# Batch 1 loaded two and three tokens a partition, with transposes, loads and copies moved, in a sliding-window attention and GEGLU kernel

## The chip, the cores and the metric

One core of one Trainium2 chip. The metric is the device time of one execution in microseconds (us). An execution takes some 1.8 us more than the span that its profile shows (366.16 us for a span of 364.4). A run is called slow here when it is over 1.5% above the fastest of its kernel; verdicts use fast runs. Clock means the clock granted to PE, the matmul engine (TensorE), as a share of full speed.

## The reference

Eight batches of attention (8 heads, 576 tokens, head size 64), with an ALiBi bias and a window of 128 tokens, feed one feed-forward block over all 4608 tokens.

```python
scores = scale * np.matmul(q, k.transpose(0, 1, 3, 2))
mask = (rel >= 0) & (rel < 128)
scores = np.where(mask, scores + bias[None], -1e9)
attn = softmax(scores)                        # shortened
x = (attn @ v) as [4608, 512]                 # shortened
return (gelu(x @ w_gate) * (x @ w_val)) @ w_out
```

## The kernel before

It works in nine groups of 512 tokens: gate and value matmuls (`gate_val`), then eight half tiles of the output product (`out_half`), among which the attention of the next batches is placed by hand. PE is meant never to stop. ACT is ScalarE, DVE is VectorE, POOL is GpSimd, SP is SyncE. Batch 0 and batch 1 are transposed by PE, batches 2 to 7 by DMA transposes that SP issues. POOL issues all loads, in program order. `bank()` gives one PSUM bank. Cuts are marked.

```python
RUNS = ((0, 128, 3), (384, 96, 2))       # batch 0: first token, partitions, tokens a partition

def transpose_runs(n, what, c, ps):      # used for batch 0
    first, parts, r = RUNS[n]
    src = runs((qs, ks)[what][0], n)
    for x in range(r):
        for i in (0, 1):
            nc.tensor.transpose(out=ps[64 * i:64 * i + 64, parts * x:parts * x + parts],
                                in_=src[:, 2 * c + i, 64 * x:64 * x + 64], ...)

def untangle(copy, n, what, c, ps): ...  # strided copy of that PSUM tile to qT or kT

def transpose(b, what, c, copy):         # used for batch 1
    ps = bank().bitcast(BF16)
    for j in range(5):
        nc.tensor.transpose(out=ps[:, 128 * j:128 * j + 128],
            in_=(qs, ks)[what][b][:, j, 128 * c:128 * c + 128], identity=ident)
    copy(out=(qT, kT)[what][b][:, :, c, :], in_=ps[:, 0:640].rearrange(...))

# ... the loop over groups
for g in range(NG):
    for b in ((), (2, 3), (4,))[g] if g < 3 else ():
        transposes_dma(b)
    if g + 2 < B:
        load_v(g + 2)
    for f in range(7 if g == 0 else 0, NF):
        gate_val(g, f)
        if g == 0 and f in (9, 11):
            for c in (0, 1) if f == 9 else (2, 3):
                for w in (0, 1):
                    transpose(1, w, c, (act, dve)[w])
        if 2 <= g < B - 1:
            ...        # sums, spread_dma(g + 1) (the trip rd, rb), transposes_dma(g + 3), values
    for b in ((3,), (4, 5))[g] if g < 2 else (g + 4,):
        if b < B:
            load_qk(b)
    for item in steps(g):
        ...            # out_half, scores, sums, spread_pe, values
```

`spread_dma` writes a row of reciprocals to DRAM (`rd`) and reads it back spread over partitions (`rb`), which the product into `xT` needs.

The softmax here doesn't subtract the row's maximum and nothing guards it: scores larger than these inputs give would overflow.

Of the kernel before, what the change touches and what calls it, by code (L numbers as in the profile page):

```python
# [7 lines left out]
FP32 = mybir.dt.float32  # L8
# [18 lines left out]
def kernel(  # L27
# [10 lines left out]
    nc = tc.nc  # L38
    B, H, S, D = q.shape
    W = 128  # L40
    NTOK = B * S
    DM = H * D
    DFF = moe_w_gate.shape[1]
    NF = DFF // 128
    NG = NTOK // 512
# [11 lines left out]
    o_pool = ctx.enter_context(tc.tile_pool(name="op", bufs=3))  # L57
# [9 lines left out]
    def bank():  # L67
        ps = psum.tile([128, 512], FP32, name="ps")
        for _ in range(heat.pop()):
            nc.tensor.matmul(out=ps, lhsT=zeros[:, 0:128], rhs=zeros, start=True, stop=True)  # L70
        heat.append(0)
        return ps

    def keep_busy(n):
# [4 lines left out]
    wo = consts.tile([128, NF, DM], BF16, name="wo")  # L79
    xT = consts.tile([128, 4, NTOK], BF16, name="xT")  # L80
    ident = consts.tile([128, 128], BF16, name="ident")
# [4 lines left out]
    qs, ks = ([consts.tile([128, 5, DM], BF16, name=f"{nm}s{i}") for i in range(2)]  # L86
              for nm in "qk")
    qT, kT = ([consts.tile([128, 5, 4, 128], BF16, name=f"{nm}T{i}") for i in range(2)]
              for nm in "qk")
# [9 lines left out]
    def load_qk(b):  # L99
        load(qs[b % 2], q, b)  # L100
        load(ks[b % 2], k, b)
# [4 lines left out]
    def runs(t, n):  # L106
        first, parts, r = RUNS[n]
        lo = 1536 * n
        return t.rearrange("p j x -> p (j x)")[0:parts, lo:lo + 512 * r].rearrange(
            "p (h x) -> p h x", h=H)  # L110

    def load_runs(n, h0, h1):
        first, parts, r = RUNS[n]
        for t, src in ((qs[0], q), (ks[0], k)):
            nc.gpsimd.dma_start(
                out=runs(t, n)[:, h0:h1, :],
                in_=src[0][h0:h1, first:first + parts * r, :].rearrange(
                    "h (p r) d -> p h (r d)", r=r))

    def load_v(b, js=range(5)):  # L120
        load(vb[b % 2], v, b, js)
# [8 lines left out]
    def by_pair(t):  # L130
        return t.rearrange("p j c t -> p (j c t)").rearrange("p (c x) -> p c x", c=4)

    def transpose_runs(n, what, c, ps):

        first, parts, r = RUNS[n]
        src = runs((qs, ks)[what][0], n)
        for x in range(r):
            for i in (0, 1):
                nc.tensor.transpose(
                    out=ps[64 * i:64 * i + 64, parts * x:parts * x + parts],  # L140
                    in_=src[:, 2 * c + i, 64 * x:64 * x + 64],
                    identity=ident[0:parts, 0:parts])

    def untangle(copy, n, what, c, ps):

        first, parts, r = RUNS[n]
        dst = by_pair((qT, kT)[what][0])[:, c, 64 + first:64 + first + parts * r]
        if isinstance(c, int):
            copy(out=dst.rearrange("p (x r) -> p x r", r=r),  # L149
                 in_=ps[:, 0:parts * r].rearrange("p (r x) -> p x r", r=r))  # L150
        else:
            n = c.stop - c.start
            copy(out=dst.rearrange("p c (x r) -> p c x r", r=r),
                 in_=ps[:, 0:n * parts * r].rearrange("p (c r x) -> p c x r", c=n, r=r))

    def transpose(b, what, c, copy):
        ps = bank().bitcast(BF16)
        for j in range(5):
            nc.tensor.transpose(
                out=ps[:, 128 * j:128 * j + 128],  # L160
                in_=(qs, ks)[what][b][:, j, 128 * c:128 * c + 128], identity=ident)
        copy(out=(qT, kT)[what][b][:, :, c, :],
             in_=ps[:, 0:640].rearrange("p (j t) -> p j t", t=128))

    def blocks(t, b, i, c, j, n):
        if b == 0:
            return by_pair(t[b])[64 * i:64 * i + 64, c, 128 * j:128 * (j + n)].rearrange(
                "p (n t) -> p n t", n=n)
        return t[b % 2][64 * i:64 * i + 64, j:j + n, c, :]
# [126 lines left out]
    hid = {}  # L296
# [25 lines left out]
    def out_half(g, u):  # L322
        t, half = u // 2, u % 2
        if half == 0:
            acc[g] = bank()
        po = acc[g]
        for f in range(6 * half, 6 * half + 6):
            nc.tensor.matmul(  # L328
                out=po, lhsT=hid[g][:, f, 128 * t:128 * (t + 1)],
                rhs=wo[:, f, :], start=(f == 0), stop=(f == NF - 1))  # L330
        if half == 1:
            osb = o_pool.tile([128, DM], FP32, name="osb")
            nc.scalar.copy(out=osb, in_=po)  # L333
            r0 = 512 * g + 128 * t
            nc.sync.dma_start(out=out[r0:r0 + 128, :], in_=osb)


    load_runs(0, 0, 4)
    zeros = consts.tile([128, 512], BF16, name="zeros")
    nc.vector.memset(zeros, 0.0)  # L340
    nc.vector.memset(ident, 0.0)
    for t in (qT[0], kT[0]):
        nc.vector.memset(by_pair(t)[:, :, 0:64], 0.0)
    nc.vector.memset(sel, 0.0)
    nc.gpsimd.affine_select(
        out=ident, in_=ident, compare_op=ALU.not_equal, fill=1.0,
        base=0, pattern=[[-1, 128]], channel_multiplier=1)
    load_runs(0, 4, 8)
    tmpl = consts.tile([128, 256], FP32, name="tmpl")
    nc.gpsimd.iota(tmpl, pattern=[[1, 256]], base=0, channel_multiplier=-1,  # L350
                   allow_small_or_imprecise_dtypes=True)
    for half, base, step, chan in ((0, 0, 1, -1), (1, -1, -1, 1)):
        t = tmpl[:, 128 * half:128 * half + 128]
        nc.gpsimd.affine_select(
            out=t, in_=t, compare_op=ALU.is_ge, fill=1e9,
            base=base, pattern=[[step, 128]], channel_multiplier=chan)
    load_runs(1, 0, 8)
    step = DFF // 4
    load_v(0, (0, 1, 2))
    load_w(0, step)  # L360
    for c in range(4):
        nc.gpsimd.affine_select(
            out=sel, in_=sel, compare_op=ALU.not_equal, fill=1.0,
# [2 lines left out]
    load_v(0, (3, 4))  # L366
    for n in (2, 3):
        load_w(step * n, step * (n + 1))
    for t in (qs[1], ks[1]):
        nc.vector.memset(t[0:64, 0, :], 0.0)  # L370
    load_qk(1)


    nc.vector.memset(ones, 0.0)
# [11 lines left out]
    act, dve = nc.scalar.copy, nc.vector.tensor_copy  # L386
    def first(cs):
        for w in (0, 1):
            if w and len(cs) == 2:
                keep_busy(1)  # L390
            for c in cs:
                ps = bank().bitcast(BF16)
                transpose_runs(0, w, c, ps)
                untangle(dve, 0, w, c, ps)

    def rest(cs):
        for w in (0, 1):
            ps = bank().bitcast(BF16)
            for k, c in enumerate(cs):
                transpose_runs(1, w, c, ps[:, 192 * k:192 * k + 192])  # L400
            untangle(act, 1, w, slice(cs[0], cs[-1] + 1), ps)

    keep_busy(8)
    first((0, 1))
# [9 lines left out]
    masks, tails = [], []  # L414
# [23 lines left out]
    for n in range(2):  # L438
        nc.gpsimd.dma_start(
            out=wo[:, 6 * n:6 * n + 6, :],  # L440
            in_=moe_w_out[768 * n:768 * n + 768, :].rearrange("(c p) f -> p c f", p=128))
    load_v(1)
    for t in (qs[0], ks[0]):
# [6 lines left out]
    todo = {  # L450
        0: [("s2", 1), ("s", 1, 0, (0, 1)), 0, 1, ("s", 1, 0, (2, 3)), 2,
            ("s", 1, 1, (0, 1), None, masks), 3, ("sum", 1, 0), ("masks",),
            ("s", 1, 1, (2, 3)), 4, ("spread", 1, 0, (act, act)), 5, ("sum", 1, 1),
            ("pv", 1, 0), 6, ("spread", 1, 1, (act, act)), ("pv", 1, 1), 7],
        1: [("s2", 2), ("s", 2, 0, (0, 1)), 0, 1, ("s", 2, 0, (2, 3)), 2,
            ("s", 2, 1, (0, 1), None, masks), 3, ("sum", 2, 0), ("masks",),
# [9 lines left out]
    def steps(g):  # L466
        b = g + 2
        if g in todo:
            return todo[g]
        if b >= B:  # L470
            return range(8)
        return [("s2", b), ("s", b, 0, (0, 1)), 0, 1, 2, ("s", b, 0, (2, 3)),
                ("s", b, 1, (0,)), 3, 4, 5, ("s", b, 1, (1, 2, 3)), 6, 7]

    def flush():
        for args in masks:
# [1 line left out]
        masks.clear()  # L478

    RUN = {"s2": scores2, "s": scores, "sum": sums, "spread": spread_pe, "pv": values,  # L480
           "masks": flush}

    for g in range(NG):
        for b in ((), (2, 3), (4,))[g] if g < 3 else ():
            transposes_dma(b)
        if g + 2 < B:
            load_v(g + 2)
        for f in range(7 if g == 0 else 0, NF):
            gate_val(g, f)
            if g == 0 and f in (9, 11):  # L490
# [4 lines that stand above are left out]
                if f == (1 if g == 2 else 0):  # L495
                    sums(g + 1, 0)
                if f == (2 if g == 2 else 0):
                    sums(g + 1, 1)
                    spread_dma(g + 1)
                    if g + 3 < B:  # L500
                        transposes_dma(g + 3)
                elif g > 2 and f in (8, 10):
                    for s in (0, 1):
                        values(g + 1, s, (f - 8, f - 7))
        for b in ((3,), (4, 5))[g] if g < 2 else (g + 4,):
            if b < B:
                load_qk(b)
        for item in steps(g):
            if isinstance(item, int):
                out_half(g, item)  # L510
            else:
                RUN[item[0]](*item[1:])
# [30 lines left out]
```

## Time and profile before

| what | where it is read | value |
|---|---|---|
| time, 6 runs beside the change | times of the runs | 362.82 us median, 361.9 to 366.68 |
| profiled run | times of the runs | 366.16 us, counted as slow (1.9% above the fastest on record, 359.2) |
| PE busy | page, part 1 | 347.5 of 364.4 us |
| PE's longest wait | waits of PE | 3.2 us, for `xT` |

The prediction shows the lines. PE is the engine that matters, so a change is worth what it removes from PE's waits. One warning that the prediction did not take seriously enough: the only profile at hand was of a slow run, and its largest wait need not be there in a fast one.

### The profile page before, as it was taken

Reading aid. Unit: us, or ns where it says so; the run is one execution under the profiler, and the core shown is the slowest. Engines: PE = TensorE matmul, PEld = TensorE weight load, DVE = VectorE, ACT = ScalarE, POOL = GpSimd, SP = SyncE. Lnnn points to the kernel's source line nnn. Section 1 sums busy time; section 2 is a strip of 40 time slices with the busy share of each in tenths; the row PEclk is TensorE's granted clock in tenths of the full one; section 3 lists DMA queues with packets and bytes.
Section 4 is the critical chain, followed back from the end, with each engine's and each line's share of the span. In section 5 each row is a group of like instructions: output and inputs, shape, how many; then the busy total and the mean of one; then the engine's idle time right before and its main releaser. Section 6 shows DMA issues by size and latency. Waiting matters only on the chain.

```text
span 364.4 us, 6688 instructions
## 1 busy us (share of the span) xinstructions
PE 347.5 (95%) x2651; PEld 172.6 (47%) x2694; DVE 185.7 (51%) x301; ACT 187.2 (51%) x341; POOL 109.1 (30%) x140
## 2 busy tenths in 40 slices
PE   7799989999999999996999999999999999999995
PEld 2468544544454445443445444444444444444442
DVE  4887458434688646372547454655474404302420
ACT  4864495536977375631683368436842223323321
POOL 8956759913783073560400040000000000000000
PEclk9999999999999999999899999999999999999999
DMA  9999999999999999999921992060205020011002
GB/s 101 176 194 172 170 170 175 174 150 155 193 188 167 121 184 145 205 172 225 144 76 39 221 109 89 31 131 0 88 33 130 2 109 6 1 59 58 0 31 86
DMA packets 151728, 42.61 MB, mean 117 GB/s; under 512 B 138856, under 2 KB 144488, under 8 KB 151696
## 3 DMA queue, kind: packets, MB, share of 16 engines
q0 software_dynamic: 112608, 18.88, 68.4%
q1 hardware_dynamic: 39088, 23.30, 31.0%
q8 instruction: 21, 0.34, 0.4%
q14 instruction: 11, 0.09, 0.1%
HBM read 43.65 MB, written 9.53 MB: 146 GB/s over the span
## 4 chain that ended last, share of the span: by engine, by line
PE 61%; DMA 27%; POOL 4%; issue 2%; SPq 2%; DVE 2%; ACT 1%; POOLq 0%; ACTq 0%; DVEq 0%
PE ps L305 31%; PE ps L328 21%; DMA qT<-qs 7%; DMA wv<-in_moe_w_val_dram 6%; DMA qs<-in_q_dram 4%; DMA wo<-in_moe_w_out_dram 4%; PE ps L180 3%; PE ps L286 3%; DMA rb<-rd 2%; DMA out_dram<-osb 2%; SPq L173 2%; DMA vb<-in_v_dram 2%; PE ps L246 2%; DVE r L255 1%; DMA rd<-r 1%
## 5 line engine op out<-in xcount | busy, mean ns | idle before, releaser
L312 DVE TENSOR_TENSOR hT<-ps,gelu 128x512 bf16<-128x512 f32 (+2 forms) x115 | 74.0, 654 | 111.8 <-PE ps L305 97.8
L311 ACT ACTIVATE gelu<-ps 128x512 bf16<-128x512 f32 (+2 forms) x115 | 65.1, 571 | 119.1 <-PE ps L305 114.7
L305 PE MATMUL ps<-xT,wg 128*128 128x512 bf16 (+2 forms) x445 | 111.8, 368 | 1.0
L305 PE MATMUL ps<-xT,wv 128*128 128x512 bf16 (+2 forms) x452 | 111.5, 367 | 0.6
L328 PE MATMUL ps<-wo,hT 128*128 128x512 bf16 x414 | 97.5, 380 | 1.6 <-DMA wo<-in_moe_w_out_dram 0.8
L187 ACT ACTIVATE P<-ps 128x512 bf16<-128x512 f32 x144 | 73.7, 623 | 7.9 <-PE ps L180 7.6
L305 PEld LDWEIGHTS <-wv 128*128 128x128 bf16 x460 | 44.9, 98 | 49.7 <-issue 1.4
L305 PEld LDWEIGHTS <-wg 128*128 128x128 bf16 x460 | 43.4, 98 | 47.7 <-issue 1.4
L190 DVE TENSOR_TENSOR P<-P,emask 128x1024 bf16<-128x1024 bf16 x72 | 48.2, 692 | 34.7 <-ACT P L187 34.7
L328 PEld LDWEIGHTS <-hT 128*128 128x128 bf16 x432 | 39.9, 98 | 50.1 <-issue 5.1
L95 POOL DMA_DIRECT2D vb<-in_v_dram x40 | 33.8, 867 | 54.2 <-PE ps L286 51.6
L95 POOL DMA_DIRECT2D qs<-in_q_dram x35 | 29.5, 857 | 42.4 <-DMA qT<-qs 29.0
L333 ACT COPY osb<-ps 128x512 f32<-128x512 f32 x36 | 21.7, 603 | 34.7 <-PE ps L328 29.5
L255 DVE RECIPROCAL r<-ps 128x320 f32<-128x320 f32 (+1 forms) x16 | 30.7, 1938 | 5.3 <-PE ps L246 5.3
L95 POOL DMA_DIRECT2D ks<-in_k_dram x35 | 29.5, 868 | 8.2 <-DMA qs<-in_q_dram 3.2
L292 DVE TENSOR_TENSOR xT<-ps,rb 128x320 bf16<-128x320 f32 (+1 forms) x64 | 24.6, 446 | 7.2 <-DMA rb<-rd 6.5
L180 PE MATMUL ps<-qT,kT 64*128 64x256 bf16 (+1 forms) x384 | 21.8, 244 | 2.8 <-DVE kT L149 1.4
L286 PE MATMUL ps<-P,vb 128*64 128x128 bf16 (+2 forms) x384 | 18.8, 247 | 3.4 <-DVE xT L292 3.2
L180 PEld LDWEIGHTS <-kT 64*128 64x128 bf16 x384 | 13.1, 94 | 14.8 <-issue 10.3
L286 PEld LDWEIGHTS <-vb 128*64 128x64 bf16 x384 | 15.2, 111 | 9.1 <-issue 8.3
L246 PEld LDWEIGHTS <-ones 128*32 128x32 bf16 x384 | 7.6, 96 | 4.9 <-issue 4.3
L246 PE MATMUL ps<-P,ones 128*32 128x128 bf16 (+2 forms) x384 | 9.9, 243 | 0.0
(50 smaller groups left out, 89.2 us busy)
## 6 DMA issues: line engine op xcount, KB each, us to landing
out_dram<-osb SPq DMA_DIRECT2D x36, 256.0 KB, 2.0
rb<-rd SPq DMA_DIRECT2D x10, 576.0 KB, 7.4
vb<-in_v_dram POOLq DMA_DIRECT2D x32, 128.0 KB, 9.0
qs<-in_q_dram POOLq DMA_DIRECT2D x28, 128.0 KB, 7.2
ks<-in_k_dram POOLq DMA_DIRECT2D x28, 128.0 KB, 6.6
wg<-in_moe_w_gate_dram POOLq DMA_DIRECT2D x4, 384.0 KB, 9.1
wv<-in_moe_w_val_dram POOLq DMA_DIRECT2D x4, 384.0 KB, 10.1
wo<-in_moe_w_out_dram POOLq DMA_DIRECT2D x2, 768.0 KB, 11.3
```

Source lines behind the costliest of these rows:

```text
L95: nc.gpsimd.dma_start(out=t[lo:128, j, :].rearrange("p (h d) -> p h d", h=H), in_=src[b][:, 128 * j - 64 + lo:128 * j + 64, :].rearrange(" ...
L180: nc.tensor.matmul(out=ps[:, col:col + 128 * n].rearrange("p (n t) -> p n t", n=n), lhsT=blocks(kT, b, i, c, j, 1).rearrange("p n t -> p ( ...
L187: nc.scalar.activation(out=dst, in_=src, func=AF.Exp, scale=0.125)
L190: nc.vector.tensor_tensor(out=dst, in0=dst, in1=m, op=ALU.mult)
L246: nc.tensor.matmul(out=ps[32 * c:32 * c + 32, a:e], lhsT=ones[:, min(j, 1), i, :], rhs=prob(b, s, c, i, j, e - a), start=(i == 0 and j == ...
L255: nc.vector.reciprocal(sumrow[b][:, lo:hi], ps[:, 0:hi - lo])
L286: nc.tensor.matmul(out=ps[64 * i:64 * i + 64, a:e], lhsT=vb[b % 2][:, j, 64 * h:64 * h + 64], rhs=prob(b, s, c, i, j, e - a), start=(j == ...
L292: nc.vector.tensor_tensor(out=xT[:, c, b * S + lo:b * S + hi], in0=ps[:, 0:hi - lo], in1=recip[b][:, c, lo:hi], op=ALU.mult)
L305: nc.tensor.matmul(out=ps[:, 0:hi - lo], lhsT=w[:, c, 128 * f:128 * (f + 1)], rhs=xT[:, c, t0 + lo:t0 + hi], start=(c == 0), stop=(c == 3))
L311: nc.scalar.activation(out=gl[:, 0:hi - lo], in_=pg[:, 0:hi - lo], func=AF.Gelu)
L312: nc.vector.tensor_tensor(out=hid[g][:, f, lo:hi], in0=pv[:, 0:hi - lo], in1=gl[:, 0:hi - lo], op=ALU.mult)
L328: nc.tensor.matmul(out=po, lhsT=hid[g][:, f, 128 * t:128 * (t + 1)], rhs=wo[:, f, :], start=(f == 0), stop=(f == NF - 1))
```

## The change

The intent: fewer and longer pieces for batch 1's loads (3,584 in place of 9,216), so that what stands behind them in POOL's queue starts sooner; batch 2's transposes earlier; batch 7's loads out of the way of batch 4's reciprocals; some work moved from ScalarE to VectorE; a shorter tail.

```diff
     def transpose(b, what, c, copy):
         ps = bank().bitcast(BF16)
-        for j in range(5):
-            nc.tensor.transpose(
-                out=ps[:, 128 * j:128 * j + 128],
-                in_=(qs, ks)[what][b][:, j, 128 * c:128 * c + 128], identity=ident)
-        copy(out=(qT, kT)[what][b][:, :, c, :],
-             in_=ps[:, 0:640].rearrange("p (j t) -> p j t", t=128))
+        for n, lo in ((0, 0), (1, 384)):
+            transpose_runs(b, n, what, c, ps[:, lo:576])
+            untangle(copy, b, n, what, c, ps[:, lo:576])
@@ out_half
-            nc.scalar.copy(out=osb, in_=po)
+            (nc.vector.tensor_copy if g < 2 and t < 2 else nc.scalar.copy)(out=osb, in_=po)
+    def out_last(g):            # the last 128 tokens, in two halves of 256 columns (cut)
@@ loads at the start
-    load_qk(1)
+    for n in (0, 1):
+        load_runs(1, n, 0, 8)
@@ steps of group 0
-            ("s", 1, 1, (2, 3)), 4, ("spread", 1, 0, (act, act)), 5, ("sum", 1, 1),
+            ("s", 1, 1, (2, 3)), 4, ("spread", 1, 0, (act, act)), 5, ("transposes", 2), ("sum", 1, 1),
@@ the loop over groups
-        for b in ((), (2, 3), (4,))[g] if g < 3 else ():
+        for b in ((), (3,), (4,))[g] if g < 3 else ():
             transposes_dma(b)
         if g + 2 < B:
             load_v(g + 2)
+        if g == 4:
+            load_qk(7)
-        for b in ((3,), (4, 5))[g] if g < 2 else (g + 4,):
-            if b < B:
-                load_qk(b)
+        for b in ((3,), (4, 5), (6,))[g] if g < 3 else ():
+            load_qk(b)
```

Cut: the batch number as an argument of the helpers, and memsets that follow from the new layout.

## The prediction

> **What bounds the kernel now.** I read the page's 40 slices first. PE is at 9 nearly throughout, so only its holes can be won back.
>
> ```profile
> PE   7799989999999999996999999999999999999995
> ...
> PEclk9999999999999999999899999999999999999999
> DMA  9999999999999999999921992060205020011002
> ```
>
> Each slice is 9.1 us. PE dips at the start, near 45 and 85 us, deepest in slice 19 (164 to 173 us), and at the end; the granted clock falls in the slice after the deepest hole. The DMA engines are full until about 180 us. Next, what PE waited for (engine, line, releaser: us in total, times, longest):
>
> ```profile
> PE ps L286 <- DVE xT L292: 3.2, 1, 3.2
> ...
> PE ps L269 <- DVE r L255: 1.3, 3, 0.5
> ...
> PE ps L328 <- DMA wo<-in_moe_w_out_dram: 0.8, 1, 0.8
> PE ps L180 <- DMA qT<-qs: 0.7, 1, 0.7
> ...
> PE ps L180 <- DVE kT L162: 0.2, 1, 0.2
> ```
>
> So after the start there is one large wait, 3.2 us, and a handful below 1 us. The windows (PE, PEld, DVE, ACT, POOL busy, then clock, DMA, GB/s) show a second cost of the large one:
>
> ```profile
> 160.00:170.00 10.00, 8.52 (x57) 4.12 (x58) 2.60 (x4) 2.71 (x5) 1.29 (x2) 1.00 1.73 199
> 170.00:180.00 10.00, 8.10 (x60) 4.06 (x61) 6.08 (x13) 4.47 (x8) 4.19 (x5) 0.83 1.52 179
> ```
>
> Clock 0.83 over 10 us means half clock for some 3.4 us, so about 1.7 us of lost work. PE's timeline agrees: the 24 value matmuls after the wait took 1.79 us, against 1.13 for the group at 163.93. Wait and slow clock cost 3.2 + 1.7 = 4.9 us in the profiled run.
>
> What causes it is in the timelines of SP, POOL and DVE (start, us, instruction):
>
> ```profile
> 136.29 7.00 SPq L173 DMA_TRANSPOSE qT<-qs  x1
> 143.38 8.27 SPq L335 DMA_DIRECT2D out_dram<-osb  x4
> 157.62 0.62 SPq L259 DMA_DIRECT2D rd<-r  x1
> 161.75 1.26 SPq L261 DMA_DIRECT2D rb<-rd  x2
> ...
> 152.75 3.51 POOL L95 DMA_DIRECT2D qs<-in_q_dram  x4 [2.12 <-DMA ks<-in_k_dram]
> ...
> 157.78 3.50 POOL L95 DMA_DIRECT2D ks<-in_k_dram  x4 [0.75 <-DMA vb<-in_v_dram]
> ...
> 171.30 1.55 DVE L292 TENSOR_TENSOR xT<-ps,rb 128x320 bf16<-128x320 f32 x4 [6.50 <-DMA rb<-rd]
> ```
>
> Batch 4's reciprocal row leaves at 157.62, comes back spread at 171.3: 13.7 us. In the next group the same trip starts at 196.64 and nothing waits for it. What differs is batch 7's q, k loads, issued by POOL at 149.95 to 161.28, in front of it. A smaller cause lies earlier: SP was busy with batch 5's transposes until 143.38, so the out stores began late, ScalarE's copy for the fourth out tile waited 2.9 us for a store, and gelu, hT and the reciprocal moved back.
>
> **What the Trainium skill says.** "DMA: Bandwidth & Descriptors", section "Issuing engines are not separate DMA queues": SP's and POOL's transfers share the same 16 engines and interleave. The trace agrees: out stores landed in 2.0 us as a median, 7.4 at worst. Same page, "Why small descriptors are slow (HBM only)": each packet has a fixed overhead. The trace agrees, but mildly: per half-us slice, the q, k, v loads in 128-byte pieces move 153 to 160 GB/s, the three-token loads of batch 0 mostly 154 to 176, weights about 200. "TensorE: Matmul & The Clock Gate", section "What's actually happening": an idle window of some 3.4 us halves the clock and a busy one restores it; that fits 3.23 us idle, then clock 0.83. "VectorE: DVE Perf Modes", section "Why PSUM operands drop a tier": fp32 from PSUM runs at single rate. The fp32 copies from PSUM below cost 1.09 ns a column, in line with that.
>
> **Batch 1 loaded in runs.** 9,216 pieces (2 x 576 x 8) become 3,584, 2 x (128 + 96) x 8, and ten issues become four. The bytes stay: 1.18 MB at 155 GB/s is 7.6 us, at 170 about 6.9. With less waiting for room in the queue I take 1 to 1.5 us earlier for all that queues behind: wo, v, batch 2. The 0.8 us wait for wo goes. On the other side, transposes and copies change:
>
> ```profile
> L162 ACT COPY qT<-ps 128x640 bf16<-128x640 bf16 x4 | 2.6, 694 | 1.1 <-PE ps L159 1.1
> ...
> L149 DVE COPY kT<-ps 128x384 bf16<-128x384 bf16 x4 | 2.1, 551 | 0.9 <-PE ps L139 0.9
> ...
> L153 ACT COPY qT<-ps 128x384 bf16<-128x384 bf16 x2 | 1.1, 554 | 0.0
> L162 DVE COPY kT<-ps 128x640 bf16<-128x640 bf16 x4 | 1.9, 486 | 0.0
> ```
>
> For PE nothing changes: five transposes take 0.28 us, and six of 128 plus four of 96 columns, in pairs, 0.17 + 0.09 by batch 0's timeline. Each copy of 640 columns becomes a strided one of 384 and one of 192: on DVE 0.55 + 0.35 (my extension of 551 ns at about 1.04 ns a column) for 0.49, on ACT 0.55 + 0.39 for 0.69. Four each: DVE +1.6, ACT +1.0 us. Half of that lies just ahead of group 0's first scores, where PE already waits 0.2 for kT. DVE starts at 46.0 and the piece needed (the third) comes out after 0.55 + 0.35 + 0.55 less overlap, near 47.35 instead of 46.9: PE loses 0.4. Net of part one: +0.8 - 0.4 = 0.4 us won.
>
> **Batch 2's transposes inside group 0.** They come before group 0's last store in SP's queue. But they began at 67.75, as batch 2's loads landed at 67.7, and SP was free at 67.4. They are bound by the loads, so the move itself gives little; the loads' 1 to 1.5 us give as much here. Of the 0.7 us wait at 87.85 I count 0.3 won, as PE also arrives 0.4 earlier. Batches 3 and 4 shift likewise, and out stores of group 1 no longer stand behind both transposes.
>
> **Batch 7's loads after group 4's V load.** They leave 150 to 161 us. The trip of 13.7 us should fall to about 9, as the next group's rd to rb issue took 1.8 us and the rb landing has a median of 7.4. It then ends near 166.5 even without an earlier start; VectorE needs it at 164.8, but PE filled its banks only at 168.6. So the 3.2 us and the slow clock after it vanish: 4.9 us in the profiled run. Their new place, about 172 to 187, has DMA to spare and the batch is not used until after 250.
>
> **Copies on VectorE.** Four of the 36 osb copies (128x512 fp32, 586 ns on ACT) go to DVE, by 485 and 415 ns for 320 and 256 columns about 695 ns. ACT is busy 9.3 of 10 us in 50 to 60, DVE 7.1: it repays the extra ACT copies. The second copy ends about when the reciprocal begins, so 0 net.
>
> **The last tile in halves.** 24 matmuls of 256 columns cost what 12 of 512 do (320 columns ran at 0.135 us each, weights hidden). The final copy drops from 586 to about 381 ns (as 256 columns have), its store has half the bytes: 0.2 + 0.15 = 0.35 us.
>
> **Sum.** 0.4 + 0.3 + 4.9 + 0.35 = 5.95 us in the profile's span (364.4 to about 358.5). The timed runs are shorter than the profiled (median 362.74, against 366.16 for the profiled run), and spread by 2 us, while PE's own work cannot vary: I take it that the large wait is smaller there, 3 us with its clock rather than 4.9. That gives 0.4 + 0.3 + 3.1 + 0.35, about 4.2: **358.6 us**, faster by 1.1%.
>
> **The rivals.**
> First: the large wait stays, because its cause is the late reciprocal and the transposes rather than batch 7's loads. For it: SP is held until 143.38 and batch 6's transposes still follow rb closely. Against: rd alone took 4.1 us to land under the loads, 1.8 from issue to the next issue without. Then only about 1 us is won: 361.5.
> Second: the freed time is given back in groups 0 and 1, where ACT and DVE pace the scores. For it: ACT at 9.3 of 10, doubled transpose copies, reciprocals that PE already waits for (1.3 us in three waits). Against: masks are done 0.5 us before PE needs them. It would add 1 to 1.5 us: about 360.
> Third: the timed runs have the large wait in full, and earlier transposes clear more of SP's queue. Then 6 to 7.3 us come off: 355.5 to 356.8, the edge of 2% (355.5).
>
> **Range and chances.** The first rival at 15% sets the upper end, the third at 20% the lower: 355.9 to 361.2. Faster by over 2% needs every hole closed: 0.08. Slower by over 2% needs a new wait of over 11 us: 0.02. Within 2%: 0.90.
>
> **What would show it.** Right: no wait of PE for xT near 168, clock 1.00 in all windows after the start, rd to the first xT product under 10 us, no wait for wo, a last ACT copy near 0.38 us. The copies of batch 1 appear as 128x384 and 128x192 with PE's wait for kT near 0.6. Wrong: xT still waits for rb over 3 us; a new wait for masks or r in groups 0 or 1; batch 7's loads delaying group 3's stores or batch 5's rb.

## The result, and the profile after

The changed kernel took **367.2 us** (median of 6, 365.96 to 367.97), against 362.82 before. The ratio is 1.010, with a 95% interval of 1.0053 to 1.0148. Ratios here are the mean time of one kernel's fast runs over that of the other's fast runs of the same rounds, so they are not quite the ratio of the medians quoted. It is slower by 1%: within 2%, but with the wrong sign and outside the range of 355.9 to 361.2.

PE by slices and its clock, from the page of the changed kernel:

```profile
PE   7799779999999999999999999999999999999996
...
PEclk9999998999999999999999999999999999999999
```

The deep hole in the middle has gone. A new one has opened in slices 5 and 6 (36 to 55 us), and the clock drops in the slice after it. What PE waited for in the changed kernel (engine, line, releaser: us in total, times, longest):

```profile
PE ps L139 <- DVE kT L149: 2.6, 4, 0.6
PE ps L139 <- ACT qT L149: 2.3, 4, 0.6
PE ps L266 <- DVE r L252: 1.3, 3, 0.5
...
PE ps L177 <- DVE kT L149: 1.0, 3, 0.5
```

The first two are new. L139 is the transpose of a run, L149 the copy that follows it. PE's timeline in the changed kernel shows the first four of the eight tiles:

```profile
40.61 0.36 PE L139 MATMUL ps<-ident,qs 128*64 128x128 bf16 x6
41.54 0.28 PE L139 MATMUL ps<-ident,qs 96*64 96x96 bf16 x4 [0.57 <-ACT qT L149]
41.62 0.36 PE L139 MATMUL ps<-ident,ks 128*64 128x128 bf16 x6
42.63 0.28 PE L139 MATMUL ps<-ident,ks 96*64 96x96 bf16 x4 [0.65 <-DVE kT L149]
42.72 0.36 PE L139 MATMUL ps<-ident,qs 128*64 128x128 bf16 x6
43.64 0.28 PE L139 MATMUL ps<-ident,qs 96*64 96x96 bf16 x4 [0.57 <-ACT qT L149]
43.73 0.36 PE L139 MATMUL ps<-ident,ks 128*64 128x128 bf16 x6
44.74 0.28 PE L139 MATMUL ps<-ident,ks 96*64 96x96 bf16 x4 [0.65 <-DVE kT L149]
45.17 0.81 PE L302 MATMUL ps<-xT,wg 128*128 128x512 bf16 x3 [0.16 <-issue]
...
73.20 1.03 PE L302 MATMUL ps<-xT,wg 128*128 128x512 bf16 x4
```

The same place in a fast run of the kernel before (e1_before, below):

```profile
41.36 0.44 PE L159 MATMUL ps<-ident,qs 128*128 128x128 bf16 x5
41.63 0.44 PE L159 MATMUL ps<-ident,ks 128*128 128x128 bf16 x5
41.91 0.44 PE L159 MATMUL ps<-ident,qs 128*128 128x128 bf16 x5
42.19 0.44 PE L159 MATMUL ps<-ident,ks 128*128 128x128 bf16 x5
42.47 1.03 PE L305 MATMUL ps<-xT,wg 128*128 128x512 bf16 x4
...
66.59 1.03 PE L305 MATMUL ps<-xT,wg 128*128 128x512 bf16 x4
```

ScalarE's timeline of the changed kernel has the copy that the second line waits for:

```profile
41.01 0.48 ACT L149 COPY qT<-ps 128x384 bf16<-128x384 bf16 x1 [0.56 <-PE ps L139]
41.85 0.32 ACT L149 COPY qT<-ps 128x192 bf16<-128x192 bf16 x1 [0.36 <-PE ps L139]
```

Read them together. PE makes six transposes of the first run, and the copy of that run starts at 41.01 and ends at 41.49. Only then, at 41.54, do the four transposes of the second run start. They write other columns, but of the same PSUM tile. Everything behind them waits as well: the next tile's transposes start only at 41.62. That happens eight times: 2.6 + 2.3 = 4.9 us of listed waits. The window that follows in the changed kernel adds the slow clock (columns as in the prediction, after the length of the window):

```profile
50.00:60.00 10.00, 8.02 (x69) 3.65 (x71) 5.03 (x9) 6.83 (x14) 10.00 (x14) 0.83 2.24 144
```

This stretch of group 0, from the first of these transposes to group 1's first gate matmul, takes 73.20 - 40.61 = 32.6 us. In the fast run of the kernel before it takes 66.59 - 41.36 = 25.2. Of the 7.4 us between them the two blocks of four tiles make 6.6: they last 4.6 (45.17 - 40.61) and 4.4 us (52.86 - 48.50), each up to the next matmul of another kind, in place of 1.1 and 1.2. So the blocks lose 1.7 us more than the listed waits: each tile's transposes come as two bursts of 0.36 and 0.28 us, in place of one stream of some 0.28 us a tile from start to start. The slow clock gives most of the rest. Read in windows of half a microsecond, it is 0.50 from 53.5 to 56.5 us, and the first twelve output matmuls take 4.1 us in place of 2.7; some 0.6 us of this is won back elsewhere.

### The profile page after: what moved, and what is told of

It reads as the page before. It is cut to its first block, busy times and chain, and to the rows that moved or that the text cites. A ratio compares the mean times of both kernels' runs of the same rounds, so it can differ in the third digit from the quotient of the medians.

```text
span 364.8 us, 6797 instructions
## 1 busy us (share of the span) xinstructions
PE 348.7 (96%) x2703; PEld 173.5 (48%) x2746; DVE 190.4 (52%) x309; ACT 186.1 (51%) x342; POOL 104.8 (29%) x136
## 4 chain that ended last, share of the span: by engine, by line
PE 85%; DVE 6%; ACT 4%; issue 2%; DMA 1%; POOL 1%; POOLq 0%; ACTq 0%; DVEq 0%
PE ps L302 48%; PE ps L325 23%; PE ps L283 5%; PE ps L177 4%; DVE r L252 3%; ACT P L184 2%; PE ps L243 2%; DMA ks<-in_k_dram 1%; PE ps L266 1%; PE ps L139 1%; DVE P L187 1%; DVE kT L149 1%; PE ps L339 1%; ACT qT L149 1%; DVE xT L289 0%
## 5 line engine op out<-in xcount | busy, mean ns | idle before, releaser
L325 PE MATMUL ps<-wo,hT 128*128 128x512 bf16 x402 | 96.1, 383 | 1.0 <-issue 0.2
L325 PEld LDWEIGHTS <-hT 128*128 128x128 bf16 x420 | 39.1, 99 | 49.2 <-issue 6.3
L330 ACT COPY osb<-ps 128x512 f32<-128x512 f32 x31 | 18.6, 601 | 29.6 <-PE ps L325 28.7
L95 POOL DMA_DIRECT2D qs<-in_q_dram x30 | 25.3, 880 | 28.8 <-DMA qT<-qs 23.3
L95 POOL DMA_DIRECT2D ks<-in_k_dram x30 | 25.5, 921 | 0.1
```

Of the source, the lines that this page charges most:

```text
L95: nc.gpsimd.dma_start(out=t[lo:128, j, :].rearrange("p (h d) -> p h d", h=H), in_=src[b][:, 128 * j - 64 + lo:128 * j + 64, :].rearrange(" ...
L325: nc.tensor.matmul(out=po, lhsT=hid[g][:, f, 128 * t:128 * (t + 1)], rhs=wo[:, f, :], start=(f == 0), stop=(f == NF - 1))
```

## The experiments

All results were correct. "Fast ratio" is against the kernel before in the same call. Each call had its own chip: the e1, e2, e3 and e4 kernels are compared most closely within a call. The kernel before was run 48, 61, 22 and 27 times beside them, with medians of 363.8, 364.27, 365.53 and 364.35 us. Of all 180 runs of the kernel before, e1_before with them, 65 count as slow; fast ratios leave these out, so they do not say whether a version has fewer of them. Where two intervals overlap, a difference is not counted as shown.

| label | kernel | median (range, runs) us | fast ratio (95% interval) |
|---|---|---|---|
| | the change | 367.2 (365.96 to 367.97, 6) | 1.010 (1.0053 to 1.0148) |
| e1_before | before, again | 363.43 (359.2 to 368.4, 22) | 0.9998 (0.9962 to 1.0034) |
| e1_order | change, transposes first, then copies | 360.89 (359.23 to 364.97, 22) | 0.9975 (0.9944 to 1.0006) |
| e1_no_runs | change without batch 1's part | 366.38 (361.15 to 367.99, 11) | 1.0044 (0.9988 to 1.0099) |
| e1_runs_only | before with batch 1's part alone | 368.99 (366.73 to 372.78, 6) | 1.0158 (1.0082 to 1.0234) |
| e2_banks | change, own bank for the second run | 361.33 (359.09 to 364.9, 22) | 0.9975 (0.9942 to 1.0009) |
| e2_undo_load7 | e1_order, batch 7's loads back | 361.95 (360.5 to 367.01, 14) | 0.9996 (0.9958 to 1.0034) |
| e2_undo_tr2 | e1_order, batch 2's transposes back | 359.5 (358.61 to 360.55, 16) | 0.9914 (0.9887 to 0.9941) |
| e2_undo_copies | e1_order, out copies on ScalarE | 361.89 (359.53 to 365.43, 22) | 0.9979 (0.9948 to 1.001) |
| e3_load7_only | before, batch 7's loads moved | 361.28 (360.18 to 363.27, 17) | 0.9922 (0.9892 to 0.9952) |
| e3_load7_back | e2_undo_tr2, batch 7's loads back | 360.22 (359.02 to 360.62, 6) | 0.9884 (0.9836 to 0.9933) |
| e3_no_runs | e2_undo_tr2 without batch 1's part | 360.5 (359.55 to 360.81, 6) | 0.9892 (0.984 to 0.9944) |
| e3_best_act | e2_undo_tr2, out copies on ScalarE | 359.06 (358.89 to 360.22, 6) | 0.9866 (0.9818 to 0.9913) |
| e4_loads_only | before with batch 1's part, mended | 360.52 (359.66 to 363.63, 22) | 0.9937 (0.9911 to 0.9963) |

### e1_before: what a fast run of the kernel before looks like

No edit.

> The kernel before, unchanged, to see what its fast runs look like, as the profile that the prediction read was of a slow run (366.16 us, against a median of 362.8). Theory F (the fast runs do not have the large wait for xT): spans near 361 us, clock near 1.00, PE's longest wait for xT under 1.5 us in a fast profile. Rival G (every run has it, and the timed ones are shorter for another reason): PE waits for xT 3 us again, clock again about 0.83 in the window that follows.

Measured: the 22 runs spread from 359.2 to 368.4, and nine count as slow. The profile fell on a fast one, with a span of 358.8. Waits of PE in it:

```profile
PE ps L269 <- DVE r L255: 1.3, 3, 0.5
...
PE ps L180 <- DVE kT L149: 1.2, 2, 0.6
...
PE ps L180 <- DVE kT L162: 0.2, 1, 0.2
```

There is no wait for `xT`, none for `wo`, and none for batch 2's `qT`. Theory F holds. VectorE's timeline shows how near it is:

```profile
167.01 1.55 DVE L292 TENSOR_TENSOR xT<-ps,rb 128x320 bf16<-128x320 f32 x4 [2.63 <-DMA rb<-rd]
```

VectorE still waits 2.63 us for `rb`, but it comes at 167.0. In the slow profile it came at 171.3, and PE had run out of banks at 168.6. So the 4.9 us that the prediction meant to win were a slow run's wait and the slow clock behind it. How many of the slow runs have this wait is not shown, as only one of them was profiled.

### e1_order: transposes first, then copies

```diff
         for n, lo in ((0, 0), (1, 384)):
             transpose_runs(b, n, what, c, ps[:, lo:576])
+        for n, lo in ((0, 0), (1, 384)):
             untangle(copy, b, n, what, c, ps[:, lo:576])
```

> The changed kernel, but with all ten transposes of a PSUM tile put ahead of its two copies. Theory A (PE waits eight times some 0.6 us until the first copy has read the tile that its next transposes write, and the clock halves after that): the waits of the transposes for the copies, 4.9 us in the changed kernel, fall to under 0.5 us, the clock stays at 1.00 and the time falls by 5.5 to 6.5 us, to about 361 us. Rival B (the strided copies and the smaller transposes themselves cost the time): the scores then wait for the copies instead, and under 3 us come back, 364.5 us or more.

Measured: 360.89 us, 6.3 below the change's median. By the two fast ratios (1.010 over 0.9975) it is 1.25%, or 4.5 us. The profiled span fell from 364.8 to 358.6. PE's timeline in this kernel, for the same four tiles and the start of the scores:

```profile
41.63 0.45 PE L139 MATMUL ps<-ident,qs 128*64 128x128 bf16 x10
41.91 0.42 PE L139 MATMUL ps<-ident,ks 128*64 128x128 bf16 x10
42.17 0.42 PE L139 MATMUL ps<-ident,qs 128*64 128x128 bf16 x10
42.42 0.42 PE L139 MATMUL ps<-ident,ks 128*64 128x128 bf16 x10
...
48.45 0.67 PE L178 MATMUL ps<-qT,kT 64*128 64x128 bf16 x10 [0.50 <-DVE kT L149]
...
66.99 1.03 PE L303 MATMUL ps<-xT,wg 128*128 128x512 bf16 x4
```

A tile now takes 0.25 to 0.28 us of PE, as five whole transposes did, and no transpose waits for a copy. The stretch of group 0 takes 66.99 - 41.63 = 25.4 us, back to the kernel before's 25.2. The doubled copies cost about what the prediction had said (0.4 us): PE waits 0.5 us for `kT` where it waited 0.2. Theory A holds in kind, and rival B falls. Two of its figures do not fit: the gain of 4.5 us by the ratios is below the 5.5 to 6.5 expected, and the clock is 1.00 in group 0 but not throughout, as it falls to 0.83 from 5 to 15 us, behind a wait of 1.53 us for the first k load. So the mean clock of the two profiles is the same (0.994 and 0.995), and only the windows show the difference. Against the kernel before, e1_order is not shown to be faster: its interval includes 1.

### e2_banks: the order kept, a bank for each run

```diff
-        ps = bank().bitcast(BF16)
         for n, lo in ((0, 0), (1, 384)):
+            ps = bank().bitcast(BF16)
             transpose_runs(b, n, what, c, ps[:, lo:576])
             untangle(copy, b, n, what, c, ps[:, lo:576])
```

> The changed kernel with the order of transposes and copies left interleaved, but the tile of the second run in a PSUM bank of its own. Theory A (what PE waits for is the read of the shared tile by the first copy, not the order or the copies themselves): as in e1_order, the waits of transposes for copies fall under 0.5 us and the median is 360 to 362 us. Rival: if it is the interleaving as such, or the sixteen copies, the waits stay near 5 us and the time near 367.

Measured: 361.33 us and the same fast ratio as e1_order, 0.9975. The waits of transposes for copies are gone from its profile; its two longest waits of PE in total are

```profile
PE ps L177 <- DMA qT<-qs: 3.8, 1, 3.8
PE ps L177 <- DVE kT L149: 1.8, 4, 0.6
```

(the first returns below). So it is the shared tile, not the interleaving or the number of copies. That the program makes PE wait is not arbitrary: the Trainium skill, "PSUM — Partial Sum Buffer", section "PSUM bank collisions raise a hardware error", says that TensorE and another engine may not touch the same bank and 32-partition quadrant at once, disjoint columns included. No run here shows a collision. The traces show the waits; whether the program puts them there for the bank or for the tile cannot be told, as each tile here is a bank of its own.

### e1_runs_only and e1_no_runs: the change taken in two

e1_runs_only is the kernel before with batch 1's part as the change has it. e1_no_runs is the change with batch 1 as before:

```diff
-    for n in (0, 1):
-        load_runs(1, n, 0, 8)
+    load_qk(1)
@@ transpose: five whole transposes and one copy again
```

> The kernel before with only the first part of the change: batch 1 in runs of 3 and 2 tokens, transposed and copied as the change does. Theory A: 5.5 to 7 us slower than before, 368.3 to 370 us, with the eight waits of PE for the copies. Rival B as well gives a loss here, so it is e1_order that tells them apart. If the loss is under 3 us, the other parts of the change bring the rest of it.

> The changed kernel without its first part: batch 1 loaded and transposed as before, everything else of the change kept. Theory A with F: 361 to 362.3 us, at most 1.8 us under the kernel before, no slow runs for want of the large wait. Rival (the prediction's term for batch 7's loads holds in the timed runs too): 358.5 us or less.

Measured: e1_runs_only 368.99 us, 5.2 above the kernel before beside it, with the eight waits (2.6 and 2.3 us) in its profile. By the fast ratio it is 1.6%, 5.7 us, as theory A had it. In this profile the clock halves between the two blocks, and for some 6.8 us instead of 3.4: the same waits were followed by different stretches of half clock.

e1_no_runs missed both expectations: 366.38 us. The rest of the change does not win what was hoped: by fast runs it is not shown to differ from the kernel before (interval 0.9988 to 1.0099). In PE's timeline of its profile (a run that counts as slow) stands:

```profile
104.03 0.61 PE L180 MATMUL ps<-qT,kT 64*128 64x128 bf16 x8 [5.24 <-DMA qT<-qs]
```

PE waits 5.24 us for batch 3's `qT`, and the clock is 0.66 in the window from 100 to 110. In the chain of work that ended last, in order of time, this wait is preceded by:

```profile
69.28 15.40 DMA ks<-in_k_dram
...
85.83 4.82 DMA qs<-in_q_dram
90.65 13.25 DMA qT<-qs
```

So there is a second culprit among the other four parts. The next runs looked for it.

### e2_undo_tr2 and e3_no_runs: batch 2's transposes put back

```diff
-            ("s", 1, 1, (2, 3)), 4, ("spread", 1, 0, (act, act)), 5, ("transposes", 2), ("sum", 1, 1),
+            ("s", 1, 1, (2, 3)), 4, ("spread", 1, 0, (act, act)), 5, ("sum", 1, 1),
@@
-        for b in ((), (3,), (4,))[g] if g < 3 else ():
+        for b in ((), (2, 3), (4,))[g] if g < 3 else ():
```

> e1_order with batch 2's transposes put back behind the last store of group 0. Theory E (in group 0 they start earlier only by as much as the loads land earlier, and put batch 3's loads back): the time stays within 0.5 us of e1_order, or the median falls by up to 1 us as fewer runs wait for batch 3's qT. Rival: the move is worth something, and the median rises by over 1 us.

> e2_undo_tr2 with batch 1 loaded, transposed and copied as in the kernel before. Theory: part one, with its order mended, is worth the prediction's 0.4 us or up to 1 us by earlier loads of wo and batch 2, so 360 to 360.7 us, with a few runs over 362 for waits on wo or batch 2's qT. Rival: it is worth nothing and the time is 359.5 us.

Measured: e2_undo_tr2 at 359.5 us, with all 16 runs within 2 us of each other and none slow; its fast ratio of 0.9914 is 0.6% (2.2 us) under that of e1_order, and of e2_banks in the same call. That is more than theory E allowed, and the rival, that the move is worth something, falls. e3_no_runs is e1_no_runs with the same edit, and falls from 366.38 to 360.5 us (fast ratios 1.0044 and 0.9892, though on different chips). Moving these transposes into group 0 costs time. SP's timeline in e1_no_runs, with the move:

```profile
62.37 6.65 SPq L173 DMA_TRANSPOSE kT<-ks  x1
69.13 7.31 SPq L173 DMA_TRANSPOSE qT<-qs  x1
...
84.75 5.79 SPq L173 DMA_TRANSPOSE kT<-ks  x1
90.65 7.73 SPq L173 DMA_TRANSPOSE qT<-qs  x1
```

and in e3_no_runs, without it:

```profile
68.14 6.14 SPq L173 DMA_TRANSPOSE kT<-ks  x1
74.39 7.07 SPq L173 DMA_TRANSPOSE qT<-qs  x1
81.69 6.65 SPq L173 DMA_TRANSPOSE kT<-ks  x1
88.44 3.65 SPq L173 DMA_TRANSPOSE qT<-qs  x1
```

With the move, batch 2's transposes start 5.8 us earlier, behind the third out store. Their loads had landed by then, so without the move it is the fourth store that holds them. Batch 3's `kT` starts 3 us later. SP was free at 77, but batch 3's k load, under way beside batch 2's transposes, took 15.4 us to land. POOL's timeline shows a second effect: `qs` comes free sooner, and batch 4's loads start at 82.68 in place of 88.55, ahead of batch 3's transposes. The last of these, `qT`, then takes 7.73 us to issue in place of 3.65, and 13.25 to land. The contention is seen in the traces; how much each of the two effects gives was not separated.

The change itself does not show this wait. Its third out store comes late, as PE is 6 us late for other reasons, and batch 2's transposes start at 68.40, no earlier than in the kernel before (68.09 in e1_before). Mending the order laid the wait open. It is not in e1_order's own profile, but it stands in three more profiles of kernels with the move: 3.8 us in e2_banks and 2.2 in e2_undo_load7, both of fast runs, and 3.7 in e2_undo_copies, of a slow one.

e3_no_runs against e3_best_act of the same call (below) is also a value for batch 1's part when mended: 360.5 against 359.06 us, fast ratios 0.9892 and 0.9866, with the out copies differing too. The intervals overlap, and e3_no_runs has none of the runs over 362 that its theory expected; what batch 1's part adds once the other parts are in is not shown.

### e2_undo_copies and e3_best_act: the out copies on ScalarE again

```diff
-            (nc.vector.tensor_copy if g < 2 and t < 2 else nc.scalar.copy)(out=osb, in_=po)
+            nc.scalar.copy(out=osb, in_=po)
```

> e1_order with all out tiles copied by ScalarE again. The prediction's term for this part was 0. Theory: within 0.5 us of e1_order. Rival: ScalarE paces groups 0 and 1, and the four copies of 0.6 us cost up to 1.2 us when given back, with longer waits of PE for the exponentials' banks or the masks.

> e2_undo_tr2 with all out tiles copied by ScalarE, the last candidate for a best version. Theory (the prediction's 0 for this part): 359.2 to 359.9 us. Rival: ScalarE paces groups 0 and 1, 360 to 361 us.

Measured: 361.89 us against e1_order's 360.89, but fast ratios of 0.9979 and 0.9975; 359.06 us against e2_undo_tr2's 359.5, on another chip. The part is worth nothing that these runs can show. e3_best_act is the best version that was run, with a span of 357.7 us: faster than the kernel before by 1.3% (interval 0.9818 to 0.9913) and than the change by more.

### e2_undo_load7, e3_load7_only, e3_load7_back, e4_loads_only: batch 7's loads

The edit of the first and third; e3_load7_only is its reverse on the kernel before, and e4_loads_only is the kernel before with only batch 1's part, in e1_order's form.

```diff
-        if g == 4:
-            load_qk(7)
@@
-        for b in ((3,), (4, 5), (6,))[g] if g < 3 else ():
+        for b in ((3,), (4, 5), (6,), (7,))[g] if g < 4 else ():
             load_qk(b)
```

> e1_order with batch 7's q, k loads put back to the end of group 3's first half, in front of batch 4's reciprocal trip. Theory C (these loads make the slow runs of the kernel before, by the wait for rb): runs of 365 us and more come back, median up by 1 to 3 us over e1_order's 360.9, and the trip from the issue of rd to the landing of rb takes 12 us or more in slow runs, against under 10 with the loads moved. Rival D (slow runs come from the loads and transposes of batches 2 and 3): the spread stays as in e1_order, 359 to 365.

> The kernel before with only batch 7's q, k loads moved behind group 4's V load. Theory C (these loads, in front of batch 4's reciprocal trip, make the slow runs of the kernel before): the runs of 365 us and more go (40% of the runs of the kernel before), the median falls from about 364 to 361 to 362 us, the fastest runs stay near 359.5 to 360.5. Rival D: the slow runs come from batches 2 and 3, then some 40% of the runs are still over 365.

> e2_undo_tr2 (359.5 us, all 16 runs between 358.6 and 360.6) with batch 7's loads put back where the kernel before has them. Theory C: runs of 363 us and more come back, and the median rises by 1 to 3 us. Rival: the spread of e2_undo_tr2 stays, because batch 1's faster loads alone removed the slow runs.

> The kernel before with only batch 1's loads in runs of 3 and 2 tokens and the order of transposes and copies mended; batch 2's transposes, batch 7's loads, the out copies and the last tile as in the kernel before. If theory C holds as it was stated (batch 7's loads alone decide), some 40% of its runs are over 364.5 us, as in the kernel before. If an earlier chain of loads is enough by itself, which the six runs of e3_load7_back hint at, no run is over 363.5 us and the median is 360.3 to 361.3 us.

Measured. On the kernel before, moving the loads alone gives 361.28 us, a fast ratio of 0.9922, and none of 17 runs above 363.3, where 13 of 22 runs of the kernel before beside it were above 364.5. Theory C seemed to hold. But e3_load7_back, with these loads back in their old place, stayed at 360.22 with no slow run in 6. That contradicts its expectation, so e4_loads_only was run: old place of the loads, old transposes, only batch 1's loads changed. It gave 360.52 us, a fast ratio of 0.9937, no slow run in 22, and one run (363.63) just above the 363.5 that was expected. e2_undo_load7 is the exception: three runs above 364, one of them slow. But it has batch 2's transposes in group 0, and its profile shows PE waiting 2.2 us for batch 3's `qT`; e1_order, with the loads moved, has four such runs of 22.

Theory C as stated, that these loads alone decide, falls. Either remedy is enough to be rid of the slow runs: a shorter queue in front of the trip, or an earlier chain of loads from batch 1 on. How the second does it is not shown. VectorE's first `xT` product of batch 4, in e3_load7_back and in e2_undo_tr2:

```profile
167.49 1.55 DVE L290 TENSOR_TENSOR xT<-ps,rb 128x320 bf16<-128x320 f32 x4 [2.58 <-DMA rb<-rd]
```

```profile
164.17 1.55 DVE L290 TENSOR_TENSOR xT<-ps,rb 128x320 bf16<-128x320 f32 x4
```

With the loads moved, `rb` is there before VectorE wants it. Without, VectorE waits 2.58 us and PE does not, and the trip from the issue of `rd` takes 167.49 - 154.71 = 12.8 us, as in e1_before's fast profile (167.01 - 154.18, with a wait of 2.63). So the early loads did not lengthen the margin in the profiles at hand. Beside them, the move is not shown to win time: 0.9914 with it and 0.9884 without, on different chips.

### The last tile, read from the traces

It needed no run of its own. From the start of the last tiles' output matmuls (line L328 before, L326 in e1_order, both right behind the last value matmul) to the end of the span, the fast kernel before takes 358.8 - 344.64 = 14.2 us and e1_order 358.6 - 344.97 = 13.6. The last copies, before and in e1_order:

```profile
355.25 0.59 ACT L333 COPY osb<-ps 128x512 f32<-128x512 f32 x1 [2.05 <-PE ps L328]
```

```profile
355.60 0.37 ACT L344 COPY osb<-ps 128x256 f32<-128x256 f32 x1 [0.94 <-PE ps L340]
```

The copy fell from 0.59 to 0.37 us, and what follows its start from 3.55 us to 3.0. The stretch is 14.2 us in e3_load7_only and e4_loads_only too, which have the old tail, and 13.6 in the change, e2_undo_tr2 and e3_best_act, which have the new one.

## Why the prediction was wrong, point by point

- **"For PE nothing changes"** is the step that failed. The prediction counted PE's matmuls (right: 0.25 to 0.28 us a tile in e1_order) and the copies (0.48 + 0.32 us on ScalarE and 0.56 + 0.36 on VectorE, near the forecast 0.55 + 0.39 and 0.55 + 0.35). It did not ask in which order they stand in the program. Transposes, copy, transposes, copy on one PSUM tile makes PE wait for each first copy: eight times some 0.6 us, 4.9 us in listed waits and 6.6 with what the broken stream of transposes loses, then a clock of 0.83 over 10 us, where twelve matmuls take 1.4 us longer. e1_order and e2_banks remove the wait in two ways and agree. The line that shows it was in the diff: `untangle` inside the loop over `n`.
- **The clock.** The Trainium skill, "TensorE: Matmul & The Clock Gate", names an idle window of 3.4 us in section "What's actually happening", and PE idling often and briefly in "A second HAM failure mode: psum-queue depth-cycling". The prediction had only the first in mind. The changed kernel looks like the second: no listed gap of PE there is over 0.65 us, PE is busy 6.71 of 10 us in the window from 40, and the clock falls behind it; without the gaps (e1_order, e2_banks) it stays at 1.00 there.
- **4.9 us for batch 7's loads** was a slow run's wait. The prediction had seen that the timed runs are shorter and cut the term to 3.1. In the fast profile of the kernel before the wait is 0, but its fast runs spread too, and in these the move alone gives 0.8% (e3_load7_only), 2.8 us: the cut term was near, by a guess, for the move alone. It is not shown to give anything more once batch 1's loads are early (e3_load7_back), so the terms could not be added. Within the change the wait did go: `rb` was late by 0.42 us for VectorE, and PE did not wait.
- **"They are bound by the loads, so the move itself gives little"**, on batch 2's transposes, misread what held them. In e1_no_runs, where batch 2's k loads are issued from 52.18 (52.71 in the profile that the prediction read), they start at 62.37 behind the third out store; so in the kernel before, at 67.75, they waited for the fourth. Where PE is on time the move takes effect, and it costs: 0.6% between e1_order and e2_undo_tr2. The prediction never asked what earlier transposes would collide with.
- **0.4 us net for batch 1's part and 0.3 for the wait at 87.85**: the waits for `wo` and `qT` are not in e1_before's profile. The second comes and goes: it is 1.6 us in e3_load7_only's profile (at 88.24) and 0.5 in e3_no_runs', both of fast runs with batch 1 loaded as before, and absent in e2_undo_tr2, e3_load7_back, e3_best_act and e4_loads_only, which load it early. So this term had a ground. Alone, with its order mended, batch 1's part gives 0.6% in fast runs (e4_loads_only).
- **0 for the out copies**: right, as far as the runs can tell.
- **0.35 us for the last tile**: right in kind, 0.5 measured.
- **The sum**: without the two faults, the order and the move of batch 2's transposes, the change gives 0.9% (e2_undo_tr2) to 1.3% (e3_best_act), where 1.1% was forecast. As the terms overlap and two were misread, that agreement is in part luck.
- Of the rivals, the second came nearest, time given back in group 0, but by waits of PE for its own transposes' copies, and about 7 us rather than 1.5. The first rival was put at 361.5 us, outside the range of up to 361.2 that it was said to set.

## What to carry to other kernels

When one engine fills a buffer in pieces and another reads it, finish the pieces before the reads begin, or give each piece its own buffer: two lines in the wrong order cost 4.5 us here by the fast ratios, about what the best version wins (1.3%, 4.9 us). Before a wait is put down as a prize, look at the spread of the times and at a profile of a fast run, as the wait may belong to some runs only. And when a transfer is moved earlier, ask what is under way at that time and what its completion sets free.

## What the Trainium skill lacked or had wrong

- "PSUM — Partial Sum Buffer" gives the rule on banks, not its price: a producer's second write of a bank behind a consumer's read of other columns cost PE 0.57 to 0.65 us each time, 4.9 us in eight, and 6.6 with the broken stream of transposes.
- "TensorE: Matmul & The Clock Gate" advises against idle gaps of over some 3 us in section "Why this matters for your kernels"; here shorter ones were followed by a window at clock 0.83: gaps of at most 0.65 us, with PE busy 6.71 of 10 us in the window from 40 (the change), and one of 2.25 us for `qT` (e2_undo_load7). Its section on the second failure mode describes the kind, without a number to plan with.
- "DMA: Bandwidth & Descriptors" gives an effective 261 GB/s for DMA transposes, measured on one kernel, in section "Latency and other measured facts"; here one of 128 x 2560 bf16 (655 KB) took 8.2 us from issue to landing in e2_undo_tr2 (80 GB/s, the time of the issue included), 13 us beside loads in e1_no_runs, and in no run less than 4.9. The page's figure is for a non-contiguous middle dimension, so the two need not be the same case.
- No page gives a figure for how much a DMA transpose and loads on the other queue slow each other: batch 3's k load took 15.4 us to land beside batch 2's transposes in e1_no_runs.
